# Three in place of four feature-tile pairs in the usual form in the first gated block

## The chip, the cores and the metric

The kernel runs on one core of one Trainium2 chip. The metric is the device time of one execution in microseconds (us), as the median of several runs. The profiled execution is a run of its own; its span, from the first to the last instruction, is shown beside the median.

## The reference

Two layers, each an attention block and a gated block, on x of 2048 tokens by 448 features; all in float32:

```python
x = A_x
for _ in range(2):
    x = x + attention(layernorm(x), A_wqkv, A_wo)      # 16 heads of 28
    n = layernorm(x)
    g, u = n @ B_w_gate, n @ B_w_up                     # 448 -> 1792
    x = x + (sigmoid(g) * u) @ B_w_down                 # 1792 -> 448
```

## The kernel before

**The gated stage.** The tokens are cut into four blocks of 512, the 1792 features into 14 tiles of 128, that is seven pairs (one tile of the lower half with one of the upper). `gated` (L1463) goes through (block b, pair p) in order; this text calls one such pass *step p* of block b. Every float32 operand is kept as the sum of two float16 parts, high and low, and each product is made of three float16 matmuls (high times high, high times low, low times high).

**Gate and up.** `gate_and_up` (L1610) multiplies the pair's gate and up weights with the block by a scheme of seven products of halves in place of eight (Winograd's form of Strassen's). TensorE runs 78 matmuls of 256 columns a step in a fixed order: `first` (into the two "chain" banks), `apart` ("side" banks), `second`, `apart`, `third`, `c11_c22`, `c21`, `c12`. ScalarE copies each chain bank out (L1625) before the next product may go into it, VectorE adds the side banks (L1641, L1648), ScalarE takes the sigmoid (L1652), VectorE multiplies (L1655). The results are `one` and `two`, the four quarters of the hidden values of this pair. Between these parts the step has six places, `along(0)` to `along(5)`, here *call 0* to *call 5*, at which other work is issued; the engines run their instructions in the order of issue, so a piece of work put into a call stands in front of what its engine has to do next for the step.

**The down product** has two forms.
- In the *usual* form (`down`, L1587), for the pairs of block 0 below `USUAL`, the hidden values are split into high and low (`hidden`, L1695) and multiplied at once: 24 matmuls of 448 columns, at the end of the step after the pair's own, into four banks that stay open over all usual pairs. `add_usual` (L1605) adds the banks to x when `AFTER_USUAL` says so: two in step 5 of block 0 (call 0), one in step 0 and one in step 2 of block 1.
- In the form of halves (`Operands`, L1495), for all other pairs, VectorE makes four sums, ScalarE seven high parts and VectorE seven low parts, all 256 columns wide: `early` and `late` in the pair's own step, `parts` and `rest` in calls 0 and 1 of the next. They go into the `hparts` tiles, and the seven products (`piece`, L1546) are made during the next block, one product a step over all such pairs: six matmuls of 224 columns for each pair. `finish` adds them to x.

**Fill steps.** While block 0 runs, blocks 1 and 2 are prepared by a queue of 29 small steps, which `portions` (L1801) hands out to (step, call). They are, in order:

| number | work |
|---|---|
| 1, 2 | norms of block 1 (VectorE statistics, GpSimd the rest) |
| 3 to 6 | `lift` of block 1: ScalarE, one 128x448 tile each (L308) |
| 7 to 10 | `square` of block 1: VectorE transposes (L316); 10 also issues the store to DRAM (L349) and the gather back (L357, L359) on SyncE |
| 11, 12 | norms of block 2 |
| 13 to 21 | `half_steps` of block 1, from the gathered data: 13 a difference on VectorE, two casts on ScalarE and a memset on GpSimd; 14 to 19 differences and low parts on VectorE and high parts on ScalarE; 20, 21 low parts and copies |
| 22 to 25 | `lift` of block 2 |
| 26 to 29 | `square` of block 2; 29 also its store and gather |

Block 2's own half steps follow from step 1 of block 1 on, and their first reads the gathered data.

**Transfers.** The gate and up weights of a pair (two of 800 KB) are loaded by GpSimd's queue two pairs ahead, when a pair's last matmul is done. `load_usual` (L1439) loads four parts a usual pair in the stage before; `load_dn` (L1447) loads a product's weights for the pairs from `USUAL` on (the products of block 0) or for all pairs (later blocks), the first three on SyncE, in block 0 after step `USUAL - 1` and step `USUAL`, into tiles two of which the usual weights have left. The down weights are prepared once, in layer 1's attention (`Prepare.split`, L1138), with an eighth form for the usual pairs.

Of the kernel before, what the change touches and what calls it, by code (L numbers as in the profile page):

```python
# [58 lines left out]

AFTER_USUAL = ((0, 5), (0, 5), (1, 0), (1, 2))  # L60
N_DN = 8
USUAL = 4
SHORT = ((10, 23, 12), (11, 24, 13), (8, 22, 9))


# [53 lines left out]
def interleaved_layers(ctx: ExitStack, tc: tile.TileContext, x_in, wqkv, wo, w_gate, w_up,  # L119
# [874 lines left out]
    class Prepare:  # L994
# [119 lines left out]
        def split(self, raw, kind, j):  # L1114
# [22 lines left out]
            else:  # L1137
                n = N_DN if j < USUAL else N_DN - 1  # L1138
                t = big.at(self.packs, "pack", [P, N_DN, 2, DN], F16)
                s12, s34 = [qrt.get("sums", [P, 2, DN]) for _ in range(2)]  # L1140
                b11, b12, b21, b22 = [v[:, z, c:c + DN] for z in (1, 0) for c in (0, DN)]
                for to, a, b in ((s12[:, 0], b12, b11), (s12[:, 1], b22, s12[:, 0]),
# [3 lines left out]
                         (t[:, 3:6:2], v[:, 0].rearrange("p (c n) -> p c n", c=2))]  # L1146
                if j < USUAL:
                    parts.append((t[:, 7], b12))
# [271 lines left out]
    class WeightsGated:  # L1420
# [18 lines left out]
        def load_usual(self):  # L1439

            self.usual = [big.get("usual", [P, 2, 4, 2, DN], F16)
                          for _ in range((USUAL + 1) // 2)]
            for p in range(USUAL):
                for i, k in enumerate((3, 5, 0, 7)):
                    nc.sync.dma_start(self.usual[p // 2][:, p % 2, i], dn_parts[k, :, p])

        def load_dn(self, queue=nc.sync):  # L1447
            t = big.get("dn", [P, NP, 2, DN], F16)
            first = USUAL if len(self.products) > NP * (NB - 1) else 0
            queue.dma_start(t[:, first:], dn_parts[self.products.popleft(), :, first:])  # L1450
# [12 lines left out]
    def gated(layer, first, wt, before_next):  # L1463
# [79 lines left out]
        def of_block(b):  # L1543
            return range(USUAL if b == 0 else 0, NP)

# [157 lines left out]
        for b, p in seq:  # L1703
# [25 lines left out]
            for i, n in enumerate(portions(b, p)):  # L1729
                at[i].append(lambda n=n: run_fill(steps, n))  # L1730
# [70 lines left out]
    def portions(b, p):  # L1801

        if b == 0:
            steps = {0: {1: 2, 2: 2, 4: 2, 5: 4}, 2: {1: 1, 2: 1, 5: 1},
                     3: {1: 1, 2: 1, 3: 1, 4: 1, 5: 1}, 4: {1: 1, 2: 1, 3: 2, 4: 2, 5: 2},
                     5: {1: 2, 2: 1}}
        elif b == 1:
            steps = {1: {1: 1, 5: 1}, 2: {5: 1}, 3: {2: 1}, 4: {1: 1, 5: 1}, 5: {1: 1, 5: 1},
                     6: {2: 1}}
        elif b == 2:  # L1810
            steps = {0: {1: 1, 2: 1}, 1: {1: 2, 2: 2, 5: 4}, 3: {5: 1}, 4: {1: 1, 2: 1, 5: 1},
                     5: {1: 1, 2: 1, 5: 1}, 6: {1: 1, 3: 1}}
        else:
            steps = {0: {1: 1, 2: 1}, 1: {1: 2, 2: 2, 5: 2}, 2: {1: 1, 2: 1, 5: 1},
                     3: {1: 1}, 4: {1: 1, 2: 1}, 5: {1: 2, 2: 2}, 6: {1: 2, 2: 2, 5: 2}}
        return [steps.get(p, {}).get(i, 0) for i in range(6)]
# [89 lines left out]
```

## Time and profile before

| | us |
|---|---|
| median of 3 runs (1894.47 to 1895.89) | 1894.67 |
| profiled execution, span | 1893.0 |
| TensorE, busy in it | 1886.5 |
| VectorE, busy | 1430.7 |
| ScalarE, busy | 1382.7 |
| GpSimd, busy | 231.5 |

The profiled execution gives its span alone; the median lies 1.67 us above it. The granted clock of TensorE is 1.000 in the span. PE is TensorE's matmuls, PEld its weight loads, DVE VectorE, ACT ScalarE, POOL GpSimd, SP SyncE. In the order in time a row has its start, the time until the last of its instructions ended, engine, line, operation, tiles and shapes, count, and, in brackets, idle time of the engine before it and what ended it. In the busy times by stretch a row has the stretch, its length, the busy time (and count) of PE, PEld, DVE, ACT and POOL, the granted clock, the share of the DMA engines and GB/s. The four blocks of layer 1's gated stage start at 600.28 us, those of layer 2's at 1536.20 us.

### The profile page before, as it was taken

To read this page: it belongs to the slowest core of one execution; us is meant where nothing else is said; L and a number is where in the kernel's file an instruction comes from. 1 tells how busy PE (TensorE), PEld (TensorE's weight loads), DVE (VectorE), ACT (ScalarE), POOL (GpSimd) and SP (SyncE) were. 2 spreads that over 40 slices of the span, in tenths; PEclk is the share of its full clock that TensorE was granted. 3 is DMA by queue.
4 is the path that set the end of the run, shared out by engine and by line. 5 is a ranking of instruction groups with operands and counts; after the bars stand their busy time and mean duration, and the time that the engine had idled before them with its cause. 6 is when DMAs were issued, how large, how long until landed. Compare 5 with 4: busy or idle time off the path is not lost. (4 is left out here: it accounts for less than half of the span.)

```text
span 1893.0 us, 56282 instructions
## 1 busy us (share of the span) xinstructions
PE 1886.5 (100%) x24254; PEld 1323.1 (70%) x24254; DVE 1430.7 (76%) x2835; ACT 1382.7 (73%) x1772; POOL 231.5 (12%) x453
## 2 busy tenths in 40 slices
PE   9999999999999999999999999999999999999999
PEld 4455555555556799999954556667666567999998
DVE  7758989898976688787564487787778676887664
ACT  5569999999993566555345799999999745565541
POOL 3023112222101111111100000000000020121110
PEclk9999999999999999999999999999999999999999
DMA  7676454334323566646734322122120245666553
GB/s 247 194 212 166 132 137 128 107 119 129 103 88 121 192 205 235 231 181 238 251 96 134 90 52 47 32 52 52 31 48 24 67 160 174 218 251 223 208 208 142
DMA packets 110882, 270.86 MB, mean 143 GB/s; under 512 B 13214, under 2 KB 67838, under 8 KB 110496
## 3 DMA queue, kind: packets, MB, share of 16 engines
q0 software_dynamic: 31776, 158.51, 23.4%
q1 hardware_dynamic: 78288, 108.20, 20.3%
q8 instruction: 192, 3.15, 0.7%
q10 hardware_dynamic: 560, 0.46, 0.1%
q14 instruction: 66, 0.54, 0.1%
HBM read 207.88 MB, written 50.85 MB: 137 GB/s over the span
## 5 line engine op out<-in xcount | busy, mean ns | idle before, releaser
L1222 ACT ACTIVATE prob_s<-sc 128x1536 f32<-128x1536 f32 (+1 forms) x657 | 887.9, 1487 | 6.6 <-PE sc L1207 5.9
L1258 PE MATMUL acc<-prob_s,val_s 128*32 128x256 f32 (+3 forms) x7700 | 569.9, 383 | 0.0
L1207 PE MATMUL sc<-qp_s 114*32 114x512 f16 x7868 | 553.2, 379 | 0.0
L579 PEld LDWEIGHTS <-gu_s 128*128 128x128 f16 x4368 | 426.9, 98 | 46.8 <-issue 0.4
L1207 PEld LDWEIGHTS <-qp_s 114*32 114x32 f16 x8192 | 272.7, 95 | 203.4 <-issue 88.3
L1258 PEld LDWEIGHTS acc<-prob_s,val_s 128*32 128x32 f32 x7700 | 272.3, 110 | 142.9 <-issue 13.6
L579 PE MATMUL chain<-xwide_s,gu_s 128*128 128x256 f16 x2016 | 247.5, 273 | 0.0
L1552 PE MATMUL dnp<-dn_s,hparts_s 128*128 128x224 f16 x2016 | 225.2, 259 | 0.0
L1552 PEld LDWEIGHTS <-hparts_s 128*128 128x128 f16 x2016 | 194.0, 98 | 4.4
L1238 DVE SCALAR_TENSOR_TENSOR power_q<-power_q,expo_q 128x512 f32<-128x512 f32 x243 | 168.2, 692 | 8.3
L1625 ACT COPY one_q<-chain 128x256 f32<-128x256 f32 x224 | 82.4, 371 | 121.4 <-PE chain L579 120.8
L1641 DVE TENSOR_TENSOR one_q<-side,one_q 128x512 f32<-128x512 f32 x112 | 72.2, 686 | 101.8 <-PE side L579 101.5
L579 PE MATMUL side<-xshort_s,gu_s 128*128 128x256 f16 x1120 | 140.5, 273 | 0.0
L564 PE MATMUL qkp<-xhl_s,wqk_s 128*128 128x512 f16 x616 | 138.1, 379 | 0.7 <-ACT wqk_s L231 0.2
L564 PEld LDWEIGHTS <-wqk_s 128*128 128x128 f16 x616 | 60.1, 98 | 69.8 <-ACT wqk_s L231 1.1
L1437 POOL DMA_DIRECT2D gu_s<-gu_parts x104 | 56.0, 538 | 430.5 <-PE side L579 424.5
L1287 DVE STREAM_TRANSPOSE oturned_q<-acc 128x512 f32<-128x512 f32 x32 | 22.9, 716 | 97.1 <-PE acc L1258 96.9
L1258 PE MATMUL acc<-power_q,val_s 128*32 128x256 f32 (+3 forms) x300 | 94.2, 396 | 0.0
L579 PE MATMUL side<-xwide_s,gu_s 128*128 128x256 f16 x672 | 91.6, 273 | 0.0
L1505 ACT CAST hparts_s<-hsums_q 128x256 f16<-128x256 f32 (+1 forms) x136 | 65.0, 494 | 30.2 <-DVE hsums_q L1517 20.2
L756 ACT ACTIVATE qkhl_q<-qkp 128x512 f16<-128x512 f32 x56 | 33.2, 593 | 71.9 <-PE qkp L564 68.3
L1652 ACT ACTIVATE one_q<-one_q 128x512 f32<-128x512 f32 x56 | 35.2, 629 | 64.3 <-DVE one_q L1641 64.3
(218 smaller groups left out, 2318.0 us busy)
## 6 DMA issues: line engine op xcount, KB each, us to landing
gu_s<-gu_parts POOLq DMA_DIRECT2D x104, 800.0 KB, 6.0
dn_s<-dn_parts POOLq DMA_DIRECT2D x42, 784.0 KB, 7.8
qp_s<-qk_scr SPq DMA_DIRECT2D x96, 224.0 KB
qk_scr<-qkhl_q SPq DMA_DIRECT2D x56, 256.0 KB
gu_parts<-pack_s POOLq DMA_DIRECT2D x14, 800.0 KB, 3.8
xt_scr<-xs_s SPq DMA_DIRECT2D x48, 224.0 KB
xraw_s<-xt_scr SPq DMA_DIRECT2D x12, 768.0 KB
qp_s<-qk_scr SPq DMA_DIRECT2D x64, 112.0 KB
```

The source lines that it names most:

```text
L564: nc.tensor.matmul(pm, w, x, start=(i == 0), stop=(i == len(terms) - 1))
L579: nc.tensor.matmul(pm, a, x, start=(first and i == 0), stop=(i == len(terms) - 1), skip_group_check=True)
L1207: nc.tensor.matmul(ps[32 * j:32 * j + 32, :], hd.k[:, keys], hd.q[:, qb * W:(qb + 1) * W], start=True, stop=True, tile_position=(0, 32 * j))
L1222: nc.scalar.activation(prob[:, 0:n, :], ps[:, 0:n, :], AF.Exp, scale=exp_scale)
L1238: nc.vector.scalar_tensor_tensor(p, p, c[k], y, op0=ALU.add, op1=ALU.mult)
L1258: nc.tensor.matmul(acc[qb * VC:(qb + 1) * VC, s], v[:, kc % TB, h, :], probs[c * NB + qb][:, s], start=(kc == 0 and a == 0), stop=(kc == N ...
L1437: queue.dma_start(self.gu[-1][m], gu_parts[p, m])
L1505: nc.scalar.copy(to[:, :, 0], a)
L1552: nc.tensor.matmul(pm, a[:, x, t], w[:, p, y], start=(begin and n == 0 and (j == 0 or alone)), stop=(n == 2), skip_group_check=True)
L1625: nc.scalar.copy(to, pm)
L1641: nc.vector.tensor_tensor(one[m], side[m], one[m], op=ALU.add)
L1652: nc.scalar.activation(out, v, AF.Sigmoid, scale=gate_scale)
```

## The change

`USUAL` goes from 4 to 3: pair 3 of block 0 takes the form of halves, so its hidden values are made into `Operands` in steps 3 and 4, its down product leaves the end of step 4, and each of the seven steps of block 1 has 24 down matmuls in place of 18. The first three loads of down weights are issued one step earlier and hold four pairs in place of three, as do the other loads for block 1; three usual pairs are loaded in place of four; pair 3's eighth weight form is not made. The fill steps of block 0 are handed out anew from step 2 on:

```diff
-USUAL = 4
+USUAL = 3
...
         if b == 0:
-            steps = {0: {1: 2, 2: 2, 4: 2, 5: 4}, 2: {1: 1, 2: 1, 5: 1},
-                     3: {1: 1, 2: 1, 3: 1, 4: 1, 5: 1}, 4: {1: 1, 2: 1, 3: 2, 4: 2, 5: 2},
-                     5: {1: 2, 2: 1}}
+            steps = {0: {1: 2, 2: 2, 4: 2, 5: 4}, 2: {1: 1, 2: 1, 3: 1, 4: 1, 5: 1},
+                     3: {1: 1, 2: 1, 3: 1, 5: 1}, 4: {1: 1, 2: 1, 3: 1, 4: 1, 5: 1},
+                     5: {1: 2, 2: 1, 5: 1}, 6: {1: 1, 2: 1}}
```

In numbers of fill steps, by step of block 0 and call (`c`):

| step | before | after |
|---|---|---|
| 0 | 1 to 10 | 1 to 10 |
| 2 | 11 c1, 12 c2, 13 c5 | 11 c1, 12 c2, 13 c3, 14 c4, 15 c5 |
| 3 | 14 to 18, c1 to c5 | 16 c1, 17 c2, 18 c3, 19 c5 |
| 4 | 19 c1, 20 c2, 21 and 22 c3, 23 and 24 c4, 25 and 26 c5 | 20 c1, 21 c2, 22 c3, 23 c4, 24 c5 |
| 5 | 27 and 28 c1, 29 c2 | 25 and 26 c1, 27 c2, 28 c5 |
| 6 | none | 29 c1 (nothing is left for c2) |

## The prediction

> **What bounds the kernel now.** I read the page first, then the busy time by steps of the gated stage, then the order in time of TensorE, ScalarE and VectorE around the end of block 0, and last SyncE's transfers.
>
> ```profile
> span 1893.0 us, 56282 instructions
> ...
> PE 1886.5 (100%) x24254; PEld 1323.1 (70%) x24254; DVE 1430.7 (76%) x2835; ACT 1382.7 (73%) x1772; POOL 231.5 (12%) x453
> ```
>
> TensorE is busy all the time, so what counts is how many us of matmuls there are and whether any of them has to wait. Below, the stretches are step 4, step 5 and step 6 of block 0 in layer 1, and step 3 in layer 2.
>
> ```profile
> 647.97:661.03 13.06, 13.06 (x104) 9.97 (x103) 7.09 (x17) 9.39 (x23) 1.06 (x2) 1.00 0.35 129
> 661.03:669.54 8.51, 8.51 (x79) 7.62 (x78) 7.42 (x16) 4.38 (x13) 0.08 (x1) 1.00 0.56 146
> 669.54:678.07 8.53, 8.53 (x80) 7.62 (x78) 7.28 (x19) 5.64 (x18) 1.06 (x3) 1.00 0.93 286
> ...
> 1570.93:1583.98 13.05, 13.05 (x105) 9.97 (x103) 8.57 (x20) 7.18 (x17) 1.05 (x2) 1.00 0.47 158
> ```
>
> The first column after the stretch is its length, then PE, PEld, DVE, ACT, POOL. Two things are to be seen. A step without usual products takes 8.52 us, one with them 13.05; and in the short steps VectorE has about 1 us to spare, in the long ones 5 to 6. The change makes step 4 a short one. Now TensorE itself, in layer 1:
>
> ```profile
> 656.49 0.35 PE L1600 MATMUL dnp<-usual_s,hhl_q 128*128 128x448 f16 x1
> ...
> 661.03 1.47 PE L579 MATMUL chain<-xwide_s,gu_s 128*128 128x256 f16 x12
> ...
> 662.99 1.47 PE L579 MATMUL chain<-xwide_s,gu_s 128*128 128x256 f16 x12
> ...
> 668.45 1.25 PE L579 MATMUL side<-xshort_s,gu_s 128*128 128x256 f16 x10
> 669.54 1.47 PE L579 MATMUL chain<-xwide_s,gu_s 128*128 128x256 f16 x12
> ...
> 671.52 1.47 PE L579 MATMUL chain<-xwide_s,gu_s 128*128 128x256 f16 x12
> ...
> 687.17 1.31 PE L1552 MATMUL dnp<-dn_s,hparts_s 128*128 128x224 f16 x12
> 688.32 1.47 PE L579 MATMUL chain<-xwide_s,gu_s 128*128 128x256 f16 x12
> ```
>
> The last column of a row is its count; starts, not lengths, give the pace, since matmuls overlap. The second chain product starts 1.96 us into step 5 (662.99 - 661.03) and 1.98 us into step 6 (671.52 - 669.54). The 0.02 is a wait, and the rows of ScalarE show for what.
>
> **The change part by part. Matmuls.** Pair 3's down product leaves block 0: 24 matmuls 448 wide, 656.49 to 661.03, 4.54 us. It comes back in block 1's steps as 42 matmuls 224 wide. Twelve of them take 688.32 - 687.17 = 1.15 us, so 42 take 4.03. TensorE saves 0.51 us a layer, if all else stays covered.
>
> [...]
>
> **ScalarE at the seam of two short steps.**
>
> ```profile
> 656.41 1.40 ACT L308 ACTIVATE lifted_q<-x,off,rs 128x448 f32<-128x448 f32 x2
> ...
> 659.24 0.75 ACT L308 ACTIVATE lifted_q<-x,off,rs 128x448 f32<-128x448 f32 x1
> ...
> 667.81 0.63 ACT L1652 ACTIVATE one_q<-one_q 128x512 f32<-128x512 f32 x1 [0.97 <-DVE one_q L1641]
> ...
> 670.80 0.42 ACT L1652 ACTIVATE two_q<-two_q 128x256 f32<-128x256 f32 x1
> 671.12 0.63 ACT L1625 COPY one_q<-chain 128x256 f32<-128x256 f32 x2
> ```
>
> In step 6 the copy of the first chain product starts only at 671.12, right behind the last sigmoid of step 5, and TensorE's second product needs that copy: there is no slack at this seam. A lift costs 0.65 us (two take 1.40, one 0.75). Today the lift in call 5 of step 4 (659.24) is followed by 4.5 us of usual products. In the new plan step 4 again has a lift in call 5 (step 24), directly between sigmoid and copy, and no usual products behind it: 0.65 of wait. The lift in call 3 and the copy before it, 0.65 + 0.4, fill the idle 0.97 at 667.81 and push 0.08 more. So step 5's second product waits 0.02 + 0.65 + 0.08 = 0.75 us. The last lift (step 25), in call 1 of step 5, lies in ScalarE's idle time (4.38 of 8.51 us busy).
>
> **VectorE in steps 5 and 6.**
>
> ```profile
> 662.25 1.27 DVE L1608 SCALAR_TENSOR_TENSOR x<-dnp,back,x 128x448 f32<-128x448 f32 x2
> 663.44 0.75 DVE L1509 TENSOR_TENSOR hparts_s<-hsums_q,hparts_s 128x256 f16<-128x256 f32 x2
> ...
> 664.44 1.69 DVE L316 STREAM_TRANSPOSE xs_s<-lifted_q 128x448 f32<-128x448 f32 x3
> 667.08 1.29 DVE L1641 TENSOR_TENSOR one_q<-side,one_q 128x512 f32<-128x512 f32 x2 [0.95 <-PE side L579]
> ...
> 670.35 0.75 DVE L1648 TENSOR_TENSOR two_q<-side,two_q 128x256 f32<-128x256 f32 x2
> ...
> 674.27 0.42 DVE L1509 TENSOR_TENSOR hparts_s<-two_q,hparts_s 128x256 f16<-128x256 f32 x1
> 675.61 1.29 DVE L1641 TENSOR_TENSOR one_q<-side,one_q 128x512 f32<-128x512 f32 x2 [0.92 <-PE side L579]
> ```
>
> From one pair of sums (667.08) a step's own work lasts until 674.27 + 0.34 = 674.61: 7.53 of 8.52 us. The usual results are still added in step 5: 1.19 us (662.25 to 663.44). A transpose is 0.56 (1.69 / 3). Today step 5 has three of them and came through because step 4 left VectorE time to get ahead. In the new plan, from step 4's sums to step 5's lie 7.53 + 1.19 + two transposes 1.12 + the 0.08 above = 9.92 us, against 8.52 + 0.75 for TensorE: the sums are 0.65 late. TensorE's next need of them is at 668.45, 0.68 after the first ends (667.08 + 0.69), so this costs some 0.05 at once. But the sums 3.27 us later (670.35), the sigmoid behind them and the copy are late too, and there the slack is nil: 0.60 at step 6's second product. From there to step 6's sums lie the last two transposes: 7.53 + 1.12 = 8.65 against 8.52, late by 0.65 + 0.13 less the 0.65 that TensorE has waited, 0.13, some 0.1 at block 1's first step, which with 24 products in place of 18 is 10.8 us long and catches up. Together 1.5, less the 0.04 that both seams have today: **1.46 a layer**. Bounds: 0 if all of it is hidden, and not below, since TensorE has only those 0.04 to give back; 2.2 if every late term is paid in full (0.75 + 0.65 + 0.65 + 0.13).
>
> **Layer 2's first fill step.** Step 13 (the first to read block 1's gathered data) moves from call 5 to call 3 of step 2.
>
> ```profile
> 1564.49 0.63 ACT L1652 ACTIVATE one_q<-one_q 128x512 f32<-128x512 f32 x1 [0.97 <-DVE one_q L1641]
> ...
> 1567.24 0.71 ACT L411 CAST xwide_s<-xraw_s 128x256 f16<-128x256 f32 x2 [0.27 <-DMA xraw_s<-xt_scr]
> 1567.86 0.61 ACT L218 CAST hhl_q<-one_q 128x512 f16<-128x512 f32 x1
> 1568.38 0.61 ACT L218 CAST hhl_q<-two_q 128x512 f16<-128x512 f32 x1
> ```
>
> ```profile
> 1565.16 0.69 DVE L1655 SCALAR_TENSOR_TENSOR one_q<-one_q,one_q 128x512 f32<-128x512 f32 x1
> 1565.77 0.42 DVE L1655 SCALAR_TENSOR_TENSOR two_q<-chain,two_q 128x256 f32<-128x256 f32 x1
> 1566.11 0.75 DVE L1648 TENSOR_TENSOR two_q<-side,two_q 128x256 f32<-128x256 f32 x2
> ...
> 1569.71 0.75 DVE L419 TENSOR_TENSOR xwide_s<-xraw_s,xwide_s 128x256 f16<-128x256 f32 x2
> 1570.38 0.75 DVE L403 TENSOR_TENSOR t_q<-xraw_s,t_q 128x256 f32<-128x256 f32 x2
> ```
>
> Here the cast already waits for the transfer, which lands at 1567.24. In call 3 it stands ahead of the sigmoid that ran at 1564.49. Then: casts to 1567.86, sigmoid and product (1564.49 to 1565.16) 0.67, second product 0.61, 0.34 on, step 14's two operations 0.67 each, sums at 1570.82; sigmoid 0.45 on, 0.32, three casts of 0.52 that stand before the copy, copy 0.37, TensorE 0.05: 1573.6. TensorE would want it at 1570.93 + 1.96 = 1572.9: a wait of **0.7**, in layer 2 alone. Bounds: 0 if the data lands 0.7 sooner, 1.5 if as much later. In layer 1 no wait for this transfer stands in the views, and I take 0.
>
> **At nothing:** steps 14 to 19, which move up within or into steps 2 and 3, where usual products cover 4.5 us (without them each would cost its 0.6 to 0.7); GpSimd's memset and the earlier loads of down weights, which wait for no VectorE work and move 112 KB more a load in block 1, in a DMA share of about 0.5 to 0.6; four small loads fewer; pair 3's eighth weight form, two operations fewer on VectorE in layer 1's attention, at most 0.9 us (0.42 each as the nearest row) under a busy TensorE; seven narrow casts and eleven narrow VectorE operations of pair 3 in place of four wide ones, which are in the 7.53.
>
> **Sum:** 2 x (1.46 - 0.51) + 0.7 = 2.6 us, from 1893.0 to 1895.6 in the profiled span. The median lies 1.67 above the span (1894.67), so 1897.2.
>
> **Rivals.** *All is covered*: TensorE's 1.02 us is won, 1893.6. For it: there is not a wait over 0.02 today. Against it: the seam at 671.12. *Weight loads set the pace* of the added products: 78 of them take 7.62 us in step 5, 98 ns each, 42 take 4.10 in place of 4.03, 2 x 0.07 more, 1897.3; the row with twelve in 1.15 us speaks against it. [...] *The second gather comes late*, the one on the slow side:
>
> ```profile
> 666.16 3.00 SPq L349 DMA_DIRECT2D xt_scr<-xs_s  x4
> 674.88 0.38 SPq L357 DMA_DIRECT2D xraw_s<-xt_scr  x1
> ...
> 1548.28 3.18 SPq L349 DMA_DIRECT2D xt_scr<-xs_s  x4
> 1562.21 0.39 SPq L357 DMA_DIRECT2D xraw_s<-xt_scr  x1
> ...
> 692.07 0.71 ACT L411 CAST xwide_s<-xraw_s 128x256 f16<-128x256 f32 x2
> ```
>
> Block 2's store and gather move from step 5 to step 6, up to GpSimd's gate load for block 1's second step. From store to gather it took 8.7 us (674.88 - 666.16), but 13.9 where two gate loads crossed it (1562.21 - 1548.28); from there to data 5.0 (1567.24). The store would follow the last transpose, at step 6's sums, 2.5 us before block 1 begins (678.07 - 675.61); the data is wanted 0.58 + 692.07 - 678.07 = 14.6 us after. With 8.7 + 5.0 it lands at 11.2, in time; with 13.9 + 5.0 at 16.4, 1.8 late. Paid in both layers it is 3.6 us more: 1900.8. It decides from a gather issued 12 us after its store. *The change does not do what it says*: VectorE bounds block 1 too and the matmuls saved there buy nothing, 2 x 0.51 more, 1898.2; the slack of longer steps speaks against it.
>
> **How the numbers follow.** Forecast 0.56, all covered 0.15, weight loads 0.03, late gather 0.20, bound by VectorE in block 1 0.04, something unseen and faster 0.02. A measurement of this kernel can tell about 0.2% (3.8 us) from no change; only the late gather is past it. So faster 0.02, same 0.78, slower 0.20. The range goes from 1893.3 (all covered, less 0.3) to 1900.2, most of the way into the late gather.
>
> **What would show it.** Right: step 4 at some 9 us or less, step 5 some 0.7 and step 6 some 0.6 us longer than 8.52, with a lift in front of the copy; a wait for the gather in step 2 of layer 2 only; block 1's steps at 10.8. Wrong: steps 4 to 6 all at 8.52; a wait for the gather in block 1's second step; or any change outside the gated stages.

## The result and the profile after

| | before | after |
|---|---|---|
| median of 5 runs each, us | 1895.43 (1894.47 to 1895.89) | 1910.02 (1908.84 to 1911.52) |
| ratio, 95% interval | | 1.0078 [1.0067, 1.009] |
| profiled execution, span, us | 1893.0 | 1908.1 |
| granted TensorE clock in it | 1.000 | 0.997 |

The change makes the kernel 0.78% slower, outside the range of the forecast. The median before is now that of five runs, 0.76 us above the one of three given earlier. First the page of the changed kernel: the span with the busy times, and from its part 4 the shares of the chain that ended last.

```profile
span 1908.1 us, 56366 instructions
...
PE 1891.0 (99%) x24290; PEld 1325.7 (69%) x24290; DVE 1436.1 (75%) x2851; ACT 1386.2 (73%) x1782; POOL 230.6 (12%) x453
...
PE 42%; DMA 1%; DVE 1%; ACT 0%; SPq 0%; issue 0%
PE acc L1258 12%; PE sc L1207 11%; PE chain L579 6%; PE dnp L1552 5%; PE side L579 4%; DMA xraw_s<-xt_scr 1%; DMA xt_scr<-xs_s 1%; PE aside L1207 1%; PE op L589 0%; PE op L590 0%; PE op L591 0%; DVE hparts_s L1509 0%; PE dnp L1602 0%; PE dnp L1600 0%; PE dnp L1601 0%; PE op L1380 0%
```

TensorE's busy time has grown by 4.5 of the 15.1 us (1891.0 - 1886.5); in the rest it is idle. And two transfers now stand in the chain that ended last: the store `xt_scr<-xs_s` and the gather `xraw_s<-xt_scr`. The busy times by step show where. These are steps 4, 5 and 6 of layer 1's block 0, steps 0, 1 and 2 of its block 1, and step 1 of block 1 in layer 2 (columns as in the prediction).

```profile
647.58:656.10 8.52, 8.52 (x80) 7.65 (x79) 4.68 (x12) 6.62 (x17) 0.09 (x1) 1.00 0.30 102
656.10:665.39 9.29, 8.75 (x80) 7.62 (x78) 8.96 (x22) 6.74 (x18) 1.06 (x3) 1.00 0.49 179
665.39:674.50 9.11, 8.74 (x81) 7.63 (x79) 8.79 (x22) 5.94 (x17) 1.06 (x3) 1.00 0.62 208
674.50:685.36 10.86, 10.86 (x104) 9.93 (x102) 9.38 (x23) 6.76 (x19) 2.02 (x4) 1.00 0.73 216
685.36:703.63 18.27, 13.86 (x105) 11.51 (x104) 9.43 (x20) 6.79 (x17) 2.14 (x4) 0.81 0.51 174
703.63:714.44 10.81, 10.81 (x104) 9.92 (x103) 8.93 (x20) 5.38 (x13) 1.60 (x3) 1.00 0.45 181
...
1629.48:1646.65 17.17, 12.64 (x105) 10.82 (x103) 9.18 (x20) 6.76 (x17) 2.13 (x4) 0.90 0.49 177
```

Step 1 of block 1 takes 18.27 and 17.17 us where its neighbour takes 10.81: 7.46 + 6.36 = 13.8 of the 15.1 us. It is also the only step of the gated stages whose granted clock is below 1 (0.81 and 0.90). Steps 5 and 6 are longer than 8.52 by 0.77 and 0.59. TensorE's rows of the changed kernel, in order of time, show what it waited for.

```profile
658.84 1.47 PE L579 MATMUL chain<-xwide_s,gu_s 128*128 128x256 f16 x12 [0.54 <-ACT one_q L1625]
...
667.24 0.82 PE L579 MATMUL side<-xwide_s,gu_s 128*128 128x256 f16 x6 [0.37 <-DVE two_q L1648]
667.95 1.47 PE L579 MATMUL chain<-xwide_s,gu_s 128*128 128x256 f16 x12
...
696.85 2.29 PE L579 MATMUL chain<-xshort_s,gu_s 128*128 128x256 f16 x10 [4.41 <-ACT one_q L1625]
...
1641.08 1.98 PE L579 MATMUL chain<-xshort_s,gu_s 128*128 128x256 f16 x10 [4.53 <-ACT one_q L1625]
```

In step 1 TensorE stands still for 4.41 us because ScalarE has not copied a chain bank out, and the ten matmuls that follow take 2.29 us (1.25 elsewhere). ScalarE in turn waited 6.60 us for the gathered data of block 2; its row and SyncE's and GpSimd's transfers, same kernel:

```profile
672.22 3.01 SPq L349 DMA_DIRECT2D xt_scr<-xs_s  x4
...
674.41 0.53 POOL L1437 DMA_DIRECT2D gu_s<-gu_parts  x1 [8.03 <-PE side L579]
...
684.13 1.07 POOL L1437 DMA_DIRECT2D gu_s<-gu_parts  x2 [8.41 <-PE side L579]
684.88 0.38 SPq L357 DMA_DIRECT2D xraw_s<-xt_scr  x1
685.82 0.54 POOL L1450 DMA_DIRECT2D dn_s<-dn_parts  x1 [0.62 <-PE dnp L1552]
...
695.81 0.71 ACT L411 CAST xwide_s<-xraw_s 128x256 f16<-128x256 f32 x2 [6.60 <-DMA xraw_s<-xt_scr]
```

The store is issued 2.28 us before block 1 begins (674.50), the gather 12.66 us after the store, and the data is there 10.9 us after that (684.88 to 695.81), 21.3 us into block 1, where the forecast put the need at 14.6. This cast (L411), the first to read block 2's data, is issued in call 1 of the step, in front of the copy that TensorE needs, which starts at 696.43, right behind it; so what of the lateness goes beyond ScalarE's slack lands on TensorE: of the 6.60 us that ScalarE waits, TensorE waits 4.41.

### The profile page after: what moved, and what is told of

Same layout as the page of the kernel before. It is cut to its first block, busy times and chain, and to the rows that moved or that the text cites. A ratio compares the mean times of both kernels' runs of the same rounds, so it can differ in the third digit from the quotient of the medians.

```text
span 1908.1 us, 56366 instructions
## 1 busy us (share of the span) xinstructions
PE 1891.0 (99%) x24290; PEld 1325.7 (69%) x24290; DVE 1436.1 (75%) x2851; ACT 1386.2 (73%) x1782; POOL 230.6 (12%) x453
## 5 line engine op out<-in xcount | busy, mean ns | idle before, releaser
L1258 PEld LDWEIGHTS acc<-prob_s,val_s 128*32 128x32 f32 x7700 | 270.6, 110 | 144.2 <-issue 13.8
L1552 PE MATMUL dnp<-dn_s,hparts_s 128*128 128x224 f16 x2100 | 237.0, 260 | 0.0
L1552 PEld LDWEIGHTS <-hparts_s 128*128 128x128 f16 x2100 | 203.0, 98 | 5.4
L579 PE MATMUL chain<-xshort_s,gu_s 128*128 128x256 f16 x560 | 72.0, 277 | 8.9 <-ACT one_q L1625 8.9
```

The costliest lines, as they stand in the source:

```text
L579: nc.tensor.matmul(pm, a, x, start=(first and i == 0), stop=(i == len(terms) - 1), skip_group_check=True)
L1258: nc.tensor.matmul(acc[qb * VC:(qb + 1) * VC, s], v[:, kc % TB, h, :], probs[c * NB + qb][:, s], start=(kc == 0 and a == 0), stop=(kc == N ...
L1552: nc.tensor.matmul(pm, a[:, x, t], w[:, p, y], start=(begin and n == 0 and (j == 0 or alone)), stop=(n == 2), skip_group_check=True)
```

## The experiments

The theory: **the gather of block 2 is late**, because the new plan moves its store from step 5 to step 6 of block 0, where store and gather cross GpSimd's weight loads (674.41, 684.13, 685.82); TensorE pays the wait and then a lowered clock. Rivals: that **three usual pairs in place of four** are the cause (shorter steps, larger loads of down weights), whatever the plan; and that **the seams** of the two short steps (the lift in front of the copy, VectorE's sums) carry most of the loss.

| run | ratio to before, 95% interval | profiled span, us |
|---|---|---|
| the change | 1.0078 [1.0067, 1.009] | 1908.1 |
| e1: store back in step 5 | 1.0013 [1.0004, 1.0022] | 1894.9 |
| e2: data read a step later | 1.001 [1.0001, 1.0019] | 1894.7 |
| e3: new plan, four usual pairs | 1.0071 [1.0055, 1.0086] | 1908.0 |
| e4: one weight load on SyncE's queue | 1.0015 [1.0006, 1.0024] | 1894.7 |
| e5: TensorE kept busy in the wait | 1.0061 [1.0046, 1.0076] | 1904.1 |
| e6: old plan, three usual pairs | 1.0032 [1.0019, 1.0046] | 1898.9 |
| e8: seams and store cleared | 0.9999 [0.999, 1.0008] | 1892.2 |
| e9: before, with 12 usual loads | 0.9999 [0.9989, 1.0009] | 1892.8 |
| e10: e2 with later sums | 1.0004 [0.9995, 1.0013] | 1894.4 |

### Store back in step 5 (e1)

```diff
-                     5: {1: 2, 2: 1, 5: 1}, 6: {1: 1, 2: 1}}
+                     5: {1: 2, 2: 1, 5: 2}}
```

> As the changed kernel, but fill step 29 (last transpose, store and gather of block 2) goes back from call 1 of step 6 to call 5 of step 5, some 2.9 us earlier. Theory A (the late gather of block 2 costs 7.4 us a layer, the rest is two seams of 0.95 net): the store now runs ahead of the gate load for block 1's second step, the gather is issued by some 2 us into block 1, nothing waits for it, block 1's step 1 takes 10.8 us and the median is 1897 (1896 to 1898.5). Rival B (three usual pairs cost the time, by 24 down products a step and larger loads in block 1): the time stays at 1905 or more.

Fill step 29 (the last transposes and the store) now closes step 5. SyncE and ScalarE of this run:

```profile
670.35 3.67 SPq L349 DMA_DIRECT2D xt_scr<-xs_s  x4
676.83 0.38 SPq L357 DMA_DIRECT2D xraw_s<-xt_scr  x1
...
689.57 0.71 ACT L411 CAST xwide_s<-xraw_s 128x256 f16<-128x256 f32 x2
```

The store is only some 2 us earlier than in the changed kernel, but the gather follows it after 6.48 us (676.83 - 670.35) in place of 12.66, and the cast waits for nothing. 1897.08 us (before 1894.98): 13 of the 15 us come back by moving one fill step.

### The data read a step later (e2)

```diff
-            steps = {1: {1: 1, 5: 1}, 2: {5: 1}, 3: {2: 1}, 4: {1: 1, 5: 1}, 5: {1: 1, 5: 1},
+            steps = {2: {1: 1, 2: 1, 5: 1}, 3: {2: 1}, 4: {1: 1, 5: 1}, 5: {1: 1, 5: 1},
```

> As the changed kernel, with store and gather where the change put them, but block 2's first half step, which reads the gathered data, moves from call 1 of step 1 of block 1 to call 1 of step 2; the half step of call 5 of step 1 moves with it. Theory A: the data lands some 21 us after block 1's start and is now wanted some 25 us after it; no wait, 1897 (1896 to 1899). Rival B: 1905 or more. Rival C (the transfers themselves slow the step, not the wait for them): step 1 of block 1 stays several us over 10.8.

```profile
672.36 3.01 SPq L349 DMA_DIRECT2D xt_scr<-xs_s  x4
685.58 0.38 SPq L357 DMA_DIRECT2D xraw_s<-xt_scr  x1
...
700.06 0.71 ACT L411 CAST xwide_s<-xraw_s 128x256 f16<-128x256 f32 x2
```

Here the transfers are as late as in the changed kernel (13.2 us from store to gather), but the first reader comes at 700.06 and finds its data. 1896.99 us. So the crossing as such costs nothing, nor does anything that it does to TensorE's weights: the late data costs time only where its first reader stands too early for it.

### The new plan with four usual pairs (e3)

```diff
-USUAL = 3
+USUAL = 4
```

> Four usual pairs as in the kernel before, with the changed kernel's plan of fill steps: the plan alone. Theory A: the store stands in step 6, the gather comes late again, 7 to 8 us a layer, 1909 to 1912; the seam of steps 4 and 5 is covered by the usual products. Rival B: 1895 to 1897.

ScalarE and TensorE of this run, layer 1 and then layer 2:

```profile
698.71 0.71 ACT L411 CAST xwide_s<-xraw_s 128x256 f16<-128x256 f32 x2 [6.53 <-DMA xraw_s<-xt_scr]
699.74 2.29 PE L579 MATMUL chain<-xshort_s,gu_s 128*128 128x256 f16 x10 [4.34 <-ACT one_q L1625]
...
1573.93 0.71 ACT L411 CAST xwide_s<-xraw_s 128x256 f16<-128x256 f32 x2 [4.14 <-DMA xraw_s<-xt_scr]
1580.22 1.47 PE L579 MATMUL chain<-xwide_s,gu_s 128*128 128x256 f16 x12 [1.06 <-ACT one_q L1625]
```

1909.18 us, as slow as the whole change, with the same waits (6.53 and 4.34 beside 6.60 and 4.41). The late gather comes from the plan of the fill steps alone, not from the number of usual pairs. (What three pairs cost with the old plan is seen in e6.) With four pairs the loads of down weights beside the gather hold 336 KB in place of 448, and the gather still takes 11.05 us (issued at 687.66), so their size isn't the cause either. The last two rows are of use below: with four usual pairs layer 2's step 13 in call 3 does wait for its gather, as the forecast said.

### One weight load on SyncE's queue (e4)

```diff
-                self.load_gu(nc.gpsimd)
+                self.load_gu(nc.sync if len(self.pairs) == 19 else nc.gpsimd)
```

> As the changed kernel, but the one gate and up load that is issued at the end of block 1's step 0 goes on SyncE's queue, behind the gather, in place of GpSimd's. Theory A with crossing queues (the gather is dragged to 10.9 us by the load on the other queue): the gather lands some 5 us after its issue, some 16 us after block 1's start, ScalarE waits about 1 us in place of 6.6, TensorE not at all and its clock stays full: 1897 to 1900. Rival: the gather takes that long by itself or by its own queue: 1908 to 1912.

The gate load that GpSimd issued at 684.13 in the changed kernel stands on SyncE's queue, behind the gather:

```profile
672.67 3.01 SPq L349 DMA_DIRECT2D xt_scr<-xs_s  x4
685.26 0.38 SPq L357 DMA_DIRECT2D xraw_s<-xt_scr  x1
...
686.36 0.95 SPq L1437 DMA_DIRECT2D gu_s<-gu_parts  x2
...
690.57 0.71 ACT L411 CAST xwide_s<-xraw_s 128x256 f16<-128x256 f32 x2 [0.92 <-DMA xraw_s<-xt_scr]
```

From store to gather it is still 12.59 us, but from gather to data 5.3 in place of 10.9. ScalarE waits 0.92, which its slack covers, and TensorE has no wait there: 1897.15 us. This separates the two legs. The store's late landing by itself costs TensorE nothing (e4), and e1 shows that the time comes back too when the first leg is shortened: TensorE waits only because both legs are long at once. That the second is doubled is due to the load beside it.

### TensorE kept busy in the wait (e5)

```diff
+            if b == 1 and p == 1:
+                def cover():
+                    pm = bank(2, "still")
+                    for _ in range(40):
+                        nc.tensor.matmul(pm[:, 0:W // 2], wt.gu[0][0][:, 0],
+                                         blks[1].wide[:, 0, 0, 0], start=True, stop=True)
+                at[3].append(cover)
```

> As the changed kernel, with 40 matmuls of 256 columns added on TensorE in block 1's step 1, in each layer, into a bank that nobody reads, just ahead of the product that waits for the late gather (added work, no part of the result). They take 4.4 us and fill the wait. Theory A with the clock (the wait of 4.4 us also takes the clock down, so that the matmuls behind it run at half speed and cost 3.0 us more a layer): the wait still ends at the same time, the clock stays full, 6 us less in all: 1904 (1903 to 1906). Rival D (the matmuls after the wait are slow because of their own waits): unchanged, 1909 to 1912.

```profile
692.71 4.53 PE L1746 MATMUL still<-xwide_s,gu_s 128*128 128x256 f16 x40
697.37 1.25 PE L579 MATMUL chain<-xshort_s,gu_s 128*128 128x256 f16 x10
```

The same stretch of the changed kernel, before, in and after the wait, by busy time and granted clock:

```profile
685.36:691.00 5.64, 5.64 (x55) 5.10 (x54) 3.90 (x8) 2.44 (x7) 1.08 (x2) 1.00 0.97 349
691.00:696.80 5.80, 1.43 (x14) 1.16 (x12) 0.76 (x2) 0.99 (x4) 0.00 (x0) 0.93 0.50 181
696.85:703.63 6.78, 6.78 (x39) 5.24 (x39) 4.75 (x10) 3.32 (x7) 1.06 (x2) 0.56 0.15 24
```

In the changed kernel the clock granted after the wait is 0.56 over 6.78 us; with the wait filled, the same ten matmuls take 1.25 us in place of 2.29 and the clock stays at 1.000. Step 1 is 15.48 us (685.80 to 701.28) in place of 18.27, though 40 matmuls were added and ScalarE still waits 6.69. The span falls by 4.0 us, and the median, 1906.26, by 3.8 in place of the 6 that were expected; the two ratios' intervals overlap, so the clock's share is read from the step: some 3 us in layer 1. That is the part of 18.27 - 10.81 = 7.46 which is not wait (4.41), 3.05. In layer 2 it is 6.36 - 4.53 = 1.8, where the expectation had 3.0 for both. Taken over shorter stretches, the granted clock of the changed kernel is 0.50 from the end of the wait at 696.85 to 702.70 in layer 1, 5.85 us, and from 1641.44 to 1644.80 in layer 2, 3.36 us. Half of each is lost, 2.9 and 1.7 us, which is what the steps show.

In the changed kernel a wait of 4.41 us is followed by a mean of 0.56 over 6.78 us, while the waits of 0.54 and 0.37 at the seams, in steps 5 and 6, leave the clock at 1.00, and two waits of nearly equal length (4.41 and 4.53) cost 3.0 and 1.8 afterwards. Which of the two layers pays more is not fixed: in e3 it is layer 2, which pays 2.9 us behind a wait of 4.13 (the two rows of ten matmuls after it take 2.29 and 2.34 us in place of 1.25, the twelve after them 2.02 in place of 1.31), and layer 1 pays 1.8 behind 4.34. What sets the length of the lowered stretch is not shown.

### The old plan with three usual pairs (e6)

```diff
-            steps = {0: {1: 2, 2: 2, 4: 2, 5: 4}, 2: {1: 1, 2: 1, 3: 1, 4: 1, 5: 1},
-                     3: {1: 1, 2: 1, 3: 1, 5: 1}, 4: {1: 1, 2: 1, 3: 1, 4: 1, 5: 1},
-                     5: {1: 2, 2: 1, 5: 1}, 6: {1: 1, 2: 1}}
+            steps = {0: {1: 2, 2: 2, 4: 2, 5: 4}, 2: {1: 1, 2: 1, 5: 1},
+                     3: {1: 1, 2: 1, 3: 1, 4: 1, 5: 1}, 4: {1: 1, 2: 1, 3: 2, 4: 2, 5: 2},
+                     5: {1: 2, 2: 1}}
```

> Three usual pairs with the fill plan of the kernel before: the other half of the change alone. Step 4 has lost its usual products but keeps eight fill steps, step 5 has three transposes. Theory A: the store stands in step 5, the gather is early; the seams cost some 2.5 us a layer less the 0.51 won: 1899 (1897 to 1901). Rival B: 1905 or more.

All waits of TensorE that add up to over 1.5 us in this run, each with its total, its times and the longest:

```profile
PE chain L579 <- ACT one_q L1625: 1.8, 2, 0.9
PE side L579 <- DVE one_q L1641: 1.7, 2, 0.8
PE side L579 <- DVE two_q L1648: 1.6, 4, 0.4
```

TensorE waits for no gather; with eight fill steps crowded into the short step 4, it waits 5.1 us at the seams in both layers together: 1901.19 us, ratio 1.0032, just above the 1897 to 1901 expected. This is the price of the seams if nothing is moved. The new plan brings these waits down to 1.8 (1.1 + 0.7 in the same view of e2, where no gather is waited for), and pays for it with the late gather. The steps grow by more than the waits shown, since the matmuls' shown times overlap at full pace (a row of twelve is 1.47 us long, and the next row starts 1.31 after it): steps 4 to 6 exceed 8.52 by 3.5 us a layer here, by 1.4 in the new plan.

### Seams and store cleared (e8)

```diff
-AFTER_USUAL = ((0, 5), (0, 5), (1, 0), (1, 2))
+AFTER_USUAL = ((1, 0), (1, 0), (1, 0), (1, 2))
...
-                     3: {1: 1, 2: 1, 3: 1, 5: 1}, 4: {1: 1, 2: 1, 3: 1, 4: 1, 5: 1},
-                     5: {1: 2, 2: 1, 5: 1}, 6: {1: 1, 2: 1}}
+                     3: {1: 1, 2: 1, 3: 1, 5: 4}, 4: {1: 1, 2: 1, 3: 1, 5: 1},
+                     5: {1: 1, 5: 2}}
```

> Three usual pairs, planned by theory A: fill steps 19 to 22 in call 5 of the long step 3, no lift in call 5 of step 4 (23, 24, 25 in calls 1 to 3, 26 in call 5), 27 in call 1 and 28, 29 in call 5 of step 5, and the two usual results that were added in step 5 are added in block 1's step 0, where VectorE has 3 us to spare. Each seam then costs some 0.1 and the store runs in step 5: 0.3 of stalls against 0.51 won a layer, 1894.5 to 1895.5, level with the kernel before or 0.4 us faster. If seams are something else than lifts and late sums: 1896.5 to 1897.5 as with the store alone moved back.

Steps 5 and 6 of block 0 and step 0 of block 1:

```profile
656.08:664.84 8.76, 8.74 (x81) 7.62 (x79) 8.44 (x21) 5.83 (x17) 1.06 (x3) 1.00 0.52 190
664.84:673.40 8.56, 8.56 (x80) 7.62 (x78) 8.24 (x20) 5.64 (x17) 1.05 (x3) 1.00 0.85 276
673.40:684.27 10.87, 10.87 (x105) 9.92 (x103) 10.47 (x26) 6.58 (x19) 2.03 (x4) 1.00 0.79 255
```

With fill steps 19 to 22 moved ahead into step 3, where usual products cover them, no lift left in call 5 of step 4, and the usual sums put into block 1, the short steps take 8.76 and 8.56 us and no gather is waited for. 1895.34 us: the same as before (0.9999). The span is 0.8 us under that of before, but 0.40 of it lies ahead of the first gated stage, which starts at 599.88 us in this execution and at 600.28 before; the rest is the matmuls' 1.0 less the 0.3 us a layer that the two steps and block 1's first still lose. So even with nearly every wait gone, three usual pairs in place of four win nothing that can be measured.

### Later sums of the usual products (e10)

```diff
-AFTER_USUAL = ((0, 5), (0, 5), (1, 0), (1, 2))
+AFTER_USUAL = ((1, 0), (1, 0), (1, 0), (1, 2))
...
-            steps = {1: {1: 1, 5: 1}, 2: {5: 1}, 3: {2: 1}, 4: {1: 1, 5: 1}, 5: {1: 1, 5: 1},
+            steps = {2: {1: 1, 2: 1, 5: 1}, 3: {2: 1}, 4: {1: 1, 5: 1}, 5: {1: 1, 5: 1},
```

> The changed kernel with the data of block 2 read a step later, as in the run that reads later, and with VectorE's sums of each fill step put behind the following step's first product, where the changed kernel has them behind the last one. The run that reads later took 1.0010 of the kernel before. If the two short steps lose their time as the forecast says, by two separate waits, then step 5 keeps its wait for ScalarE's lift (about 0.75 us, both halves of 0.3 to 0.55) and step 6's wait for VectorE falls from some 0.6 us to at most 0.2: about 0.5 us less a layer, 1.0 in all, a ratio of 1.0005 and some 1896.0. If the VectorE wait is only the tail of ScalarE's lateness a step earlier, both stay and the ratio stays at 1.0010. If the sums put later make the next product's lift late instead, step 6 grows, and the ratio is 1.0015 or more.

Steps 5 and 6 of this run, and then the same two of e2:

```profile
657.32:666.60 9.28, 8.74 (x80) 7.62 (x78) 8.43 (x22) 7.08 (x20) 1.05 (x3) 1.00 0.48 179
666.60:675.13 8.53, 8.53 (x81) 7.62 (x79) 8.24 (x20) 5.60 (x17) 1.06 (x3) 1.00 0.67 223
```

```profile
656.24:665.53 9.29, 8.75 (x80) 7.61 (x78) 8.96 (x22) 6.74 (x18) 1.05 (x3) 1.00 0.49 179
665.53:674.64 9.11, 8.74 (x81) 7.63 (x79) 8.79 (x22) 5.95 (x17) 1.06 (x3) 1.00 0.63 208
```

The edit moves less than the text above says: the first two sums of the usual products (`add_usual`) go from step 5 of block 0 to step 0 of block 1, and no fill step's sums move. That alone, VectorE's work in step 5 falling from 8.96 to 8.43 us, takes 0.58 us from step 6 and leaves step 5 as it was. The two seams are two separate waits, as the forecast had them: VectorE's sums in step 6, and in step 5 a wait for ScalarE that these sums don't touch. That the latter is the lift is read from e8, whose plan has no lift there and whose step 5 takes 8.76. The ratio, 1.0004, cannot be told from e2's 1.001; the step lengths can. The spans differ by 0.3 us only, since this execution comes to layer 1's block 0 1.08 us later than e2's (601.11 against 600.03), after a longer wait of TensorE at the kernel's start (2.9 us in place of 0.3).

### The kernel before with twelve usual loads (e9)

```diff
-                for i, k in enumerate((3, 5, 0, 7)):
+                nc.sync.dma_start(self.usual[p // 2][:, p % 2, 0:2],
+                                  dn_parts[3:6:2, :, p].rearrange("k p h n -> p k h n"))
+                for i, k in ((2, 0), (3, 7)):
```

> The kernel before, with its four usual pairs and its old plan, and with the usual pairs' gate and up weights fetched in 12 transfers in place of 16 on SyncE (two of each pair's are merged into one). The question is why layer 2's first gather, which the forecast had landing too late for the usual plan of three pairs, came early instead. If the number of SyncE's small loads sets when GpSimd's next gate load starts, that load starts some 8.45 us after layer 2's block 0 in place of 10.7 and layer 2's store to gather takes about 6.9 us in place of 13.9, with no change of time (1895, within 0.2 per cent). If it is the shorter first steps of three pairs that move the gate load, both stay at 10.7 and 13.9.

Layer 2 in this run, then in the changed kernel:

```profile
1546.68 1.25 POOL L1437 DMA_DIRECT2D gu_s<-gu_parts  x2 [4.41 <-PE chain L579]
1548.08 3.37 SPq L349 DMA_DIRECT2D xt_scr<-xs_s  x4
1561.61 0.38 SPq L357 DMA_DIRECT2D xraw_s<-xt_scr  x1
```

```profile
1552.46 1.24 POOL L1437 DMA_DIRECT2D gu_s<-gu_parts  x2 [2.10 <-PE side L579]
1556.16 3.27 SPq L349 DMA_DIRECT2D xt_scr<-xs_s  x4
1563.01 0.39 SPq L357 DMA_DIRECT2D xraw_s<-xt_scr  x1
```

Block 0 starts at 1535.93 in this run and at 1544.01 in the changed kernel, so the gate load stands at 10.75 and at 8.45 us, and store to gather takes 13.53 and 6.85. Twelve loads in place of sixteen change nothing: the idea fell. The 8.45 us stand in every run with three usual pairs, whatever its plan, and the 10.75 in every run with four, e3 too. Why the gate load comes 2.3 us earlier with three stays open.

## Why the prediction was wrong

**The step that failed** is the second gather. The forecast's sum puts it at nothing, as landing 8.7 + 5.0 us after its store, in time; the rival "the second gather comes late" is what happened, and the prediction gave it 0.20 and priced it at 1.8 us a layer. It cost 7.46 and 6.36. The rival's place was right (block 1's second step, the sign of being wrong that the prediction names), and so was the moment of the store: 2.28 us before block 1 where it says 2.5. Three numbers in it were not.
- *The gather's own leg* was put at 5.0 us, from a row where no gate load stood beside it (1562.21 to 1567.24). It took 10.9: in the new plan the gather is issued 0.75 us after a gate load of 1600 KB and 0.9 before 448 KB of down weights. e4 takes the gate load away and has 5.3. The prediction counted the crossing on the leg of the store, where it took the choice between 8.7 and 13.9, and not on the gather's.
- *What it decides from*, "a gather issued 12 us after its store", was nearly right for ScalarE (12.59 in e4, a wait of 0.92) but not for TensorE: there the same delay cost nothing. The rival took data 1.8 us late for a wait of 1.8 us of TensorE, but ScalarE's slack takes up 2.2 (6.60 - 4.41), so at the rival's 16.4 us there would have been no wait at all. With 12.66 + 10.9 the data is there 21.3 us into block 1.
- *The price* of a wait was taken as the wait alone. Behind some 4.5 us of idle TensorE the clock was half for a while: 3.0 and 1.8 us, together 4.8 of the 13.8.

The chance was too small as well. The new plan puts the last transpose, and so the store, into step 6, and a gate load is issued whenever a pair's last matmul is done: that one would cross the store and the next the gather followed from the plan. The 8.7 us were weak evidence for the other side, since there the gate load came later behind the store. In six runs, layer 1, the time from store to gather was 12.20 us (e3), 12.59 (e4), 12.66 (the change) and 13.22 (e2) with the load 2.19 behind the store, 8.72 with 3.30 (before) and 6.48 with 4.53 (e1).

**Right, by the runs.** *Matmuls*: a step of block 1 before the change, in the busy times by stretch,

```profile
688.32:698.57 10.25, 10.25 (x99) 9.38 (x98) 8.35 (x20) 6.21 (x16) 2.13 (x4) 1.00 0.53 195
```

is 10.25 us long, after it 10.81 to 10.82 (703.63 to 714.44): 7 x 0.57 = 4.0 more, and step 4 is 4.54 shorter: 0.5 saved, as forecast. That is 95 ns for each of the 42 matmuls, where the row of twelve before the change gave 96 and the rival of the weight loads 98. *The seams*: step 5 at 9.29 us where the forecast's sum gives 8.52 + 0.75 = 9.27, step 6 at 9.11 where it gives 9.12, and block 1's step 0 longer by 0.04 (forecast 0.1). By the starts, the second product of step 5 comes 2.74 us into the step (658.84 - 656.10) and that of step 6 2.56 (667.95 - 665.39), 0.78 and 0.60 more than the 1.96; the forecast has 0.75 and 0.60. In step 6 TensorE waits for VectorE directly as well (667.24), one product ahead of the copy that the forecast names. Two small readings of the prediction are off without effect: 0.65 late against 0.68 of slack costs nothing and not 0.05, and VectorE's spare time in the long step of layer 2 is 4.5 us and not 5 to 6. e1, e2 and e4, in which TensorE waits for no gather, have spans 1.7 to 1.9 us over that of before, where the forecast without the 0.7 of layer 2 is 1.9. e10 shows that they are two waits. *The rest at nothing*: steps 0 to 3 of block 0 are as long as before, and TensorE has no other wait but the short ones at the kernel's start that it has before too.

**Right for another kernel.** The 0.7 us of layer 2's first fill step did not come, because its store to gather took 6.85 us and not the 13.9 of before. In e3, with four usual pairs, it is there (1.06 us). The mechanism was right, its input changed with the number of pairs, and by what is open (e9).

**Not tried**: a gather on another queue; and the load of down weights moved by itself, so that its own share in the 10.9 us is not shown.

## What to carry to other kernels

When a store and the gather behind it move, lay both legs over the other queue's loads at their new times and price each leg at what it took in company; here a leg measured alone, 5.0 us, became 10.9. A wait on the engine that bounds the kernel is priced with what follows it, and behind 4.1 to 4.5 us of it there stood here another 1.8 to 3.0 us of lowered clock. Put the first reader of a transfer where a late one still finds slack: one step later in the plan (e2) was worth as much as an earlier transfer (e1): 1896.99 us against 1897.08.

## What the runs showed of the hardware

In the one stretch counted here, two transfers in flight on different queues did not move alike by bytes. It is the changed kernel's, counted from the trace's DMA packets by start time, per us:

```
us        GpSimd's queue     SyncE's queue
          KB    packets      KB    packets
688       268   51            60   30
689       275   44            90   45
690       270   51           104   52
691       286   50            98   49
692        91   26           276  140
693         7    2           238  140
```

From 689 to 691 each queue gets about as many packets (44 to 52 a us), but GpSimd's hold 5 to 6 KB on average and SyncE's 2 KB, so the gather moves some 95 KB a us beside the loads and some 260 once they have ended. In e4, where the load is issued behind the gather on the same queue, the gather takes 5.3 us; all queues together move 228 GB/s in these (685.26 to 690.57) and 333 in the 5.43 us after.

Equal packet counts are not the whole of it. The gather's first packet of data starts 3.30 us after its issue in the changed kernel (688.18) and 1.06 in layer 2 of the kernel before (1563.27), where no gate load stands beside it and it takes 5.0 us, so some 2 of the 5.9 us between 10.9 and 5.0 pass before the gather moves anything. And the store, in packets of 0.5 KB, which had moved some 160 KB a us alone, falls to between 2 and 76 beside the load of 674.41, with packet counts far from equal (51 against 31 at 677, 6 against 43 at 678, 152 against 48 at 679), and still to some 13 when the load has ended (684). What holds both back there is open.
